# A transformer block on one core: the half-head attention product moved next to the modulation rows, and the last output chunk cut into two pieces in place of three

## The chip, the cores and the metric

The kernel runs on one core of one Trainium2 chip. The metric is the device time of one execution in microseconds. Every run whose state is on record is in the fast state, with a mean granted clock of the tensor engine of 0.999 or 1.0. PE is the tensor engine, PEld its weight loads, DVE the vector engine, ACT the scalar engine, POOL the general engine and SP the engine that issues most of the DMA transfers (SPq is its queue).

The *span* of a run goes from its first to its last instruction in the profile. The *time outside the span* is the measured time less the span.

## The reference

```python
B, N, D = (2, 256, 1152)          # two sequences of 256 tokens, H = 2 heads of 576, F = 4 * D
mod = (_silu(c) @ w_mod).reshape(B, 6, 1, D)
shift_a, scale_a, gate_a, shift_m, scale_m, gate_m = [mod[:, i] for i in range(6)]
h = _layernorm(x, axis=-1) * (1 + scale_a) + shift_a
qkv = (h @ wqkv).reshape(B, N, 3, H, Dh)
q, k, v = ...
attn = _softmax(jnp.einsum('bqhd,bkhd->bhqk', q, k) * Dh ** (-0.5), axis=-1)
a = jnp.einsum('bhqk,bkhd->bqhd', attn, v).reshape(B, N, D) @ wo
x = x + gate_a * a
h2 = _layernorm(x, axis=-1) * (1 + scale_m) + shift_m
m = _gelu(h2 @ w_fc1) @ w_fc2
return x + gate_m * m
```

A head has 576 columns, four blocks of 128 and one half block of 64. The two half blocks share columns 512 to 639 of V: that is the "half-head" part.

## The kernel before

The kernel has its own list scheduler. PE's units run in the order in which the program lists them; the other engines' units are placed by it. `mm` is a matmul, `S.unit` opens a unit, `dma` issues a transfer, on SP unless told otherwise. These are the parts that the change touches, and what it moves them around (cuts are marked with `...`):

```python
# issue loop: the waits for older stores stand ahead of the LAST store
outs = [ins for u in order["sp"] for ins in u.instrs if ins.is_out]
last_out = outs[-1]
...
        if ins is last_out:
            for o in outs[:-4]:
                eng_handle.wait_ge(dma_sems[o.dma_sem], o.dma_val)
        bi = ins.fn(eng_handle)
...

def v_proj(t, ci):                       # V for 128 tokens and 384 columns: 9 matmuls
    ...
    for kt in range(KT):
        mm(o, HX[:, kt, t*128:(t+1)*128], WV[:, kt, ci*CH:(ci+1)*CH], kt == 0, kt == KT-1)
    copy_on("act", V[:, t, ci*CH:(ci+1)*CH], o, ...)

def rows():                              # modulation rows, tiles of 32 columns
    for kt in range(KT):
        for r in range(2):
            for j in range(4):
                mm(psum[32*j:32*j+2, ...], ST[:, kt:18:9], WMODR[...], ..., tile_position=(0, 32*j))
    ...                                  # copy out, store to DRAM, load the gate back on all partitions

def pv_halves():                         # half-head P x V, tiles of 64 columns
    for b in range(2):
        for kjt in range(2):
            for h in range(2):
                base = PVB[b][2] * 512
                mm(psum[64*h:64*h+64, base:base+256], V[:, 2*b+kjt, 512+64*h:576+64*h],
                   PTS[2*b+h][:, kjt, :], kjt == 0, kjt == 1, tile_position=(0, 64*h))
    ...                                  # two copies out of PSUM to OT

# order of the units on PE
... v_proj(2, 0); rows(); ... v_proj(2, 1); v_proj(2, 2); v_proj(3, 0); rows_T(); v_proj(3, 1); v_proj(3, 2); ...
pv_halves()
for b in range(2):
    for h in range(2):
        pv(b, h)                         # the full-width part of P x V
...

# second feed-forward product, the output; CH = 384, JT = 36
for t in range(4):
    pieces = [(0, CH), (CH, 2*CH), (2*CH, 3*CH)]
    if t == 3:
        pieces = [(0, CH), (CH, 2*CH), (2*CH, 3*CH-160), (3*CH-160, 3*CH-64), (3*CH-64, 3*CH)]
    for (c0, c1) in pieces:
        for j in range(JT):
            mm(o, GT[j][:, t*128:(t+1)*128], WFC2[:, j, c0:c1], j == 0, j == JT-1)
        # DVE: times the gate, plus x1; then the store
        ...
```

Of the kernel before, what the change touches and what calls it, by code (L numbers as in the profile page):

```python
# [171 lines left out]
class Sched:  # L172
# [225 lines left out]
    def emit(self, nc, sems, dma_sems):  # L398
# [64 lines left out]
        outs = [ins for u in order["sp"] for ins in u.instrs if ins.is_out]  # L463
        last_out = outs[-1]

        def run_engine(e, eng_handle):
            for u in order[e]:
                for ins in u.instrs:
                    for (k, v) in waits[ins.gidx]:
                        if k[0] == "d":  # L470
                            eng_handle.wait_ge(dma_sems[k[1]], v)
                        else:
                            eng_handle.wait_ge(sems[k[1]], v)
                    if ins is last_out:
                        for o in outs[:-4]:
                            eng_handle.wait_ge(dma_sems[o.dma_sem], o.dma_val)
                    bi = ins.fn(eng_handle)
                    if ins.dma_sem is not None:
                        bi.then_inc(dma_sems[ins.dma_sem], 16)
                    else:  # L480
                        bi.then_inc(sems[e], 1)
            if e == "sp":
                for o in outs[-4:-1]:
                    eng_handle.wait_ge(dma_sems[o.dma_sem], o.dma_val)
                eng_handle.wait_ge(dma_sems[last_out.dma_sem], last_out.dma_val)
# [21 lines left out]
CH = 384  # L507
# [34 lines left out]
def build_kernel(nc, x, c, wqkv, wo, w_mod, w_fc1, w_fc2, out):  # L542
# [5 lines left out]
    with (  # L548
# [377 lines left out]
        def proj(W, j, dst_j, H, bank):  # L926
            S.unit("pe", KT * c_mm(512), "qk_%d" % dst_j)
            for kt in range(KT):
                mm(ps32(bank), W[:, kt, j * 128:(j + 1) * 128], H[:, kt, :], kt == 0, kt == KT - 1)
            qk_evac(dst_j, bank)  # L930
# [84 lines left out]
        def pt_transposes(b, h):  # L1015
            idx = b * 2 + h
            bank = s_bank[(b, h)]
            S.unit("pe", 4 * c_mm(128), "PT_%d_%d" % (b, h))
            for kjt in range(2):
                for jq in range(2):  # L1020
                    tr(ps16(bank, kjt * 256 + jq * 128, 128), PP[idx][:, jq, kjt * 128:(kjt + 1) * 128], IDENT)
            copy_on("dve" if b == 0 else "act", PTS[idx].rearrange("p j k -> p (j k)"), ps16(bank, 0, 512), 512, True, "PT_ev%d" % idx)
# [4 lines left out]
        def v_proj(t, ci):  # L1027
            bank = v_banks[v_rr[0] % 3]
            v_rr[0] += 1
            S.unit("pe", KT * c_mm(CH), "v_%d_%d" % (t, ci))  # L1030
            o = ps32(bank, 0, CH)
            for kt in range(KT):
                mm(o, HX[:, kt, t * 128:(t + 1) * 128], WV[:, kt, ci * CH:(ci + 1) * CH], kt == 0, kt == KT - 1)
            copy_on("act", V[:, t, ci * CH:(ci + 1) * CH], o, CH, False, "v_ev%d_%d" % (t, ci))
# [5 lines left out]
        def rows():  # L1040
            S.unit("pe", KT * 2 * c_mm(RW) + 100.0, "rows")
# [3 lines that stand above are left out]
                        c0 = 2 * RW * j + RW * r  # L1045
                        bank = (3, 4)[r]
                        mm(psum[32 * j:32 * j + 2, bank * 512:bank * 512 + RW], ST[:, kt:18:9], WMODR[:, kt, c0:c0 + RW],
                           kt == 0, kt == KT - 1, tile_position=(0, 32 * j))
            for r, eng in ((0, "act"), (1, "dve")):
                copy_on(eng, ROWS[0:98, ROWP + r * RW:ROWP + (r + 1) * RW], ps32(3 + r, 0, RW)[0:98, :], RW, False, "rows_ev%d" % r)  # L1050
            for j in range(2):
                dma(scratch[0, :, 2 * RW * j:2 * RW * (j + 1)], ROWS[32 * j:32 * j + 2, ROWP:ROWP + 2 * RW], 2 * 2 * RW * 2, "st_ga%d" % j, eng="pool")
            gate_load(0, GA)
# [58 lines left out]
        def pv_halves():  # L1112
            S.unit("pe", 4 * c_mm(256) + 100.0, "PVh")
# [3 lines that stand above are left out]
                        base = PVB[b][2] * 512  # L1117
                        mm(psum[64 * h:64 * h + 64, base:base + 256], V[:, 2 * b + kjt, 512 + 64 * h:576 + 64 * h], PTS[2 * b + h][:, kjt, :],
                           kjt == 0, kjt == 1, tile_position=(0, 64 * h))
            for b, eng in ((0, "dve"), (1, "act")):  # L1120
                copy_on(eng, OT[:, 4, b * 256:(b + 1) * 256], ps32(PVB[b][2], 0, 256), 256, False, "OT_ev%d_4" % b)

# [84 lines left out]
        proj(WQ, 7, 7, HX, 1)  # L1207
        s_and_softmax(1, 0)
        proj(WQ, 8, 8, HX, 2)
        v_proj(0, 0)  # L1210
        s_and_softmax(0, 1)
        v_proj(0, 1)
        s_and_softmax(1, 1)
        v_proj(0, 2)
        pt_transposes(0, 0)
        v_proj(1, 0)
        pt_transposes(1, 0)
        v_proj(1, 1)
        pt_transposes(0, 1)
        v_proj(1, 2)  # L1220
        pt_transposes(1, 1)
        v_proj(2, 0)
        rows()
        wfc1_load(0)
        wfc1_load(1)
        v_proj(2, 1)
        v_proj(2, 2)
        v_proj(3, 0)
        rows_T()
        v_proj(3, 1)  # L1230
        v_proj(3, 2)
        wfc1_load(2)
        wfc1_load(3)

# [3 lines left out]
        dma(WGM, wmod_v[:, :, 5 * D:6 * D], D * D * 2, "ld_gm", run=2304)  # L1238
        wfc2_load(0)
        wfc2_load(1)  # L1240
        pv_halves()
        for b in range(2):
            for h in range(2):
                pv(b, h)
# [26 lines left out]
        for t in range(4):  # L1271
            b = t // 2
            pieces = [(0, CH), (CH, 2 * CH), (2 * CH, 3 * CH)]
            if t == 3:
                pieces = [(0, CH), (CH, 2 * CH), (2 * CH, 3 * CH - 160), (3 * CH - 160, 3 * CH - 64), (3 * CH - 64, 3 * CH)]
            for (c0, c1) in pieces:
                w = c1 - c0
                S.unit("pe", JT * c_mm(w), "fc2_%d_%d" % (t, c0))
                o = ps32(acc_bank(), 0, w)
                for j in range(JT):  # L1280
                    mm(o, GT[j][:, t * 128:(t + 1) * 128], WFC2[:, j, c0:c1], j == 0, j == JT - 1)
                gm, t1, ost, x1c = GM[b][:, c0:c1], T1[oi % 3][:, 0:w], OST[oi % 3][:, 0:w], X1[:, t, c0:c1]
                oi += 1
                dve(c_dve_psum32(w), lambda e, o=o, gm=gm, t1=t1: e.tensor_tensor(out=t1, in0=o, in1=gm, op=ALU.mult), [o, gm], [t1], "fc2_t1_%d_%d" % (t, c0))  # L1284
                dve(c_dve_32(w), lambda e, t1=t1, x1c=x1c, ost=ost: e.tensor_tensor(out=ost, in0=t1, in1=x1c, op=ALU.add), [t1, x1c], [ost], "fc2_out_%d_%d" % (t, c0))  # L1285
                dma(outv[b, :, t % 2, c0:c1], ost, P * w * 2, "st_out_%d_%d" % (t, c0), is_out=True)
# [74 lines left out]
```

## Time and profile before

| | before |
|---|---|
| time, median of 3 runs | 243.87 us (243.79 to 244.35) |
| time of the profiled run, and its span | 243.62 us, 242.3 us |
| PE busy | 238.4 us, 98% |
| last pieces, PE time (DVE start to DVE start) | 224 columns 3.45, 96 columns 1.53, 64 columns 1.23 us |
| start of the first long PE stage (K products) | 11.18 us after the span's start |

In a timeline a line reads: start, length, engine, source line, operation, shape out and in, count, and in square brackets the idle time of the engine before it with what ended that.

### The profile page before, as it was taken

To read this page: it belongs to the slowest core of one execution; us is meant where nothing else is said; L and a number is where in the kernel's file an instruction comes from. 1 tells how busy PE (TensorE), PEld (TensorE's weight loads), DVE (VectorE), ACT (ScalarE), POOL (GpSimd) and SP (SyncE) were. 2 spreads that over 40 slices of the span, in tenths; PEclk is the share of its full clock that TensorE was granted. 3 is DMA by queue.
4 is the path that set the end of the run, shared out by engine and by line. 5 is a ranking of instruction groups with operands and counts; after the bars stand their busy time and mean duration, and the time that the engine had idled before them with its cause. 6 is when DMAs were issued, how large, how long until landed. Compare 5 with 4: busy or idle time off the path is not lost.

```text
span 242.3 us, 4076 instructions
## 1 busy us (share of the span) xinstructions
PE 238.4 (98%) x1763; PEld 147.5 (61%) x1763; DVE 120.3 (50%) x218; ACT 67.0 (28%) x136; POOL 21.2 (9%) x39
## 2 busy tenths in 40 slices
PE   7999999999999999999999999999999999999996
PEld 2698854556667666898444444444566656656676
DVE  3814388696997699789999500000022222111112
ACT  5820350355424107973233322222000000000000
POOL 1400000000021186400000000020000000000000
PEclk9999999999999999999999999999999999999999
DMA  6999999999996999989953498012000000000001
GB/s 241 330 381 392 391 392 391 397 413 405 391 356 196 351 395 391 391 266 394 314 164 82 150 320 313 0 29 72 0 16 19 16 16 19 16 16 16 19 24 27
DMA packets 30140, 51.59 MB, mean 213 GB/s; under 512 B 1703, under 2 KB 15787, under 8 KB 30123
## 3 DMA queue, kind: packets, MB, share of 16 engines
q1 hardware_dynamic: 29680, 50.14, 58.0%
q0 software_dynamic: 416, 1.19, 1.6%
q8 instruction: 14, 0.23, 0.4%
q14 instruction: 3, 0.02, 0.0%
q10 hardware_dynamic: 27, 0.00, 0.0%
HBM read 50.14 MB, written 1.19 MB: 212 GB/s over the span
## 4 chain that ended last, share of the span: by engine, by line
PE 97%; DVE 2%; POOL 0%; issue 0%; ACT 0%; DVEq 0%; POOLq 0%
PE psum L688 95%; PE psum L691 2%; DVE arena L739 1%; DVE arena L760 0%; POOL arena L711 0%; DVE arena L740 0%; DVE arena L1284 0%; DVE arena L1285 0%; POOL arena L710 0%; ACT arena L726 0%; DVE arena L727 0%; DVE arena L732 0%; DVE arena L742 0%; POOL arena L717 0%; POOL arena L715 0%
## 5 line engine op out<-in xcount | busy, mean ns | idle before, releaser
L688 PE MATMUL psum<-arena 128*128 128x384 bf16 (+10 forms) x1674 | 234.9, 306 | 1.6 <-POOL arena L711 1.5
L688 PEld LDWEIGHTS psum<-arena 128*128 128x128 bf16 (+3 forms) x1674 | 142.3, 97 | 90.0 <-issue 3.8
L1079 DVE SCALAR_TENSOR_TENSOR arena<-arena 128x1152 f32<-128x1152 bf16 x32 | 44.7, 1414 | 0.6
L1284 DVE TENSOR_TENSOR arena<-psum,arena 128x384 f32<-128x384 f32 (+3 forms) x14 | 7.0, 501 | 68.0 <-PE psum L688 68.0
L1193 ACT ACTIVATE arena<-psum 128x512 bf16<-128x512 f32 (+1 forms) x44 | 22.4, 520 | 42.7 <-PE psum L688 42.7
L683 ACT ACTIVATE arena<-psum 128x512 bf16<-128x512 f32 (+6 forms) x37 | 19.6, 549 | 39.5 <-PE psum L688 37.1
L685 DVE CAST arena<-psum 128x512 bf16<-128x512 f32 (+3 forms) x13 | 8.2, 641 | 11.4 <-PE psum L688 11.3
L669 POOL DMA_DIRECT2D dit_scratch<-arena x3 | 1.8, 616 | 115.7 <-DVE arena L685 58.9
L1161 POOL TENSOR_TENSOR arena<-arena 128x384 f32<-128x384 f32 x12 | 10.9, 910 | 10.8 <-DVE arena L1160 9.5
L1106 DVE CAST arena<-psum 72x32 bf16<-72x32 f32 x1 | 0.2, 186 | 21.3 <-PE psum L688 21.3
L739 DVE BATCH_NORM_STATS2 arena<-arena 128x6 f32<-128x384 f32 (+1 forms) x18 | 9.5, 552 | 0.1
L1166 ACT ACTIVATE arena<-arena 128x1152 bf16<-128x1152 f32 x4 | 5.3, 1345 | 11.9 <-DVE arena L1165 11.9
L691 PEld LDWEIGHTS psum<-arena 128*128 128x128 bf16 (+1 forms) x89 | 5.8, 98 | 2.5 <-issue 0.8
L1160 DVE TENSOR_TENSOR arena<-psum,arena 128x384 f32<-128x384 f32 x12 | 6.5, 549 | 1.6 <-DMA arena<-dit_scratch 1.6
L1285 DVE TENSOR_TENSOR arena<-arena 128x384 bf16<-128x384 f32 (+3 forms) x14 | 7.0, 501 | 0.5
L691 PE MATMUL psum<-arena 128*128 128x128 bf16 (+1 forms) x89 | 7.1, 219 | 0.1
L1180 DVE TENSOR_SCALAR arena<-psum,arena 128x128 bf16<-128x128 bf16 x20 | 5.4, 341 | 1.9 <-PE psum L691 1.9
L1183 ACT ACTIVATE arena<-psum,arena 128x128 bf16<-128x128 bf16 x16 | 6.0, 456 | 0.9 <-PE psum L688 0.6
L1086 DVE TENSOR_REDUCE arena<-arena 128x36 f32<-128x1152 f32 x4 | 5.4, 1348 | 0.0
L1083 DVE STREAM_TRANSPOSE arena<-arena 128x1152 f32<-128x1152 f32 x4 | 5.4, 1364 | 0.0
L1009 ACT ACTIVATE arena<-psum,arena 128x256 bf16<-128x256 f32 x8 | 3.7, 472 | 1.3 <-PE psum L688 0.9
L743 POOL TENSOR_TENSOR arena<-arena 128x1 f32<-128x1 f32 x6 | 3.6, 596 | 2.0 <-DVE arena L742 2.0
(48 smaller groups left out, 44.9 us busy)
## 6 DMA issues: line engine op xcount, KB each, us to landing
arena<-in_w_fc_dram SPq DMA_DIRECT2D x9, 1152.0 KB, 7.3
arena<-in_w_fc_dram SPq DMA_DIRECT2D x4, 2592.0 KB, 17.2
arena<-in_wqkv_dram SPq DMA_DIRECT2D x18, 288.0 KB, 10.2
arena<-in_w_mod_dram SPq DMA_DIRECT2D x3, 1728.0 KB, 20.2
arena<-in_w_mod_dram SPq DMA_DIRECT2D x3, 864.0 KB, 13.7
arena<-in_w_mod_dram SPq DMA_DIRECT2D x9, 288.0 KB, 10.5
arena<-in_wqkv_dram SPq DMA_DIRECT2D x1, 2592.0 KB, 16.6
arena<-in_wo_dram SPq DMA_DIRECT2D x1, 2592.0 KB, 24.4
```

Of the source, the lines that this page charges most:

```text
L683: act(c_act(n), lambda e: e.activation(out=dst, in_=src, func=ACTF.Copy), [src], [dst], name)
L685: dve(c_dve_psum16(n) if psum16 else c_dve_psum32(n), lambda e: e.tensor_copy(dst, src), [src], [dst], name)
L688: S.instr(lambda e: e.matmul(o, lhsT=l, rhs=r, start=st, stop=sp, **kw), reads=[l, r], writes=[o])
L691: S.instr(lambda e: e.transpose(o, i_, idn), reads=[i_, idn], writes=[o])
L739: dve(550, lambda e, s=s, o=o: e.bn_stats(out=o, in_=s), [s], [o], "bn_%s_%d" % (tag, ci))
L1079: dve(1270, lambda e, w=w, s=s, acc=acc: e.scalar_tensor_tensor(out=acc, in0=w, scalar=s, in1=acc, op0=ALU.mult, op1=ALU.add), [w, s, acc] ...
L1160: dve(550, lambda e, o=o, ga=ga, x1c=x1c: e.tensor_tensor(out=x1c, in0=o, in1=ga, op=ALU.mult), [o, ga], [x1c], "wo_t1_%d_%d" % (t, ci))
L1161: S.op("pool", 930, lambda e, xs=xs, x1c=x1c: e.tensor_tensor(out=x1c, in0=x1c, in1=xs, op=ALU.add), reads=[x1c, xs], writes=[x1c], name=" ...
L1183: act(440, lambda e, o=o, dst=dst, s1=s1, s2=s2: e.activation(out=dst, in_=o, func=ACTF.Identity, scale=s1, bias=s2), [o, s1, s2], [dst], ...
L1193: act(c_act(ntok), lambda e: e.activation(out=dst, in_=o, func=ACTF.Gelu_apprx_tanh), [o], [dst], "gelu_%d_%d" % (f, tok0))
L1284: dve(c_dve_psum32(w), lambda e, o=o, gm=gm, t1=t1: e.tensor_tensor(out=t1, in0=o, in1=gm, op=ALU.mult), [o, gm], [t1], "fc2_t1_%d_%d" % ( ...
L1285: dve(c_dve_32(w), lambda e, t1=t1, x1c=x1c, ost=ost: e.tensor_tensor(out=ost, in0=t1, in1=x1c, op=ALU.add), [t1, x1c], [ost], "fc2_out_%d ...
```

## The change

The intent: the two stages in which PE works in column tiles are put side by side, so that PE switches its tiling fewer times. For that the columns of V that the half-head product reads are made first. The last output chunk is cut once, not twice, which saves 36 matmuls. The waits for older stores go ahead of the second-last store, so that they don't lie between the last two.

```diff
@@ issue loop
-                    if ins is last_out:
+                    if ins is outs[-2]:
                         for o in outs[:-4]:
                             eng_handle.wait_ge(dma_sems[o.dma_sem], o.dma_val)
@@ pv_halves
+
+        def pv_halves_ev():
             for b, eng in ((0, "dve"), (1, "act")):
                 copy_on(eng, OT[:, 4, b * 256:(b + 1) * 256], ps32(PVB[b][2], 0, 256), 256, False, "OT_ev%d_4" % b)
@@ order of the units (cut: the softmax and transpose units, which keep their slots, and the removed lines of the moved v_proj and rows_T)
+        v_proj(0, 1)
+        v_proj(1, 1)
+        v_proj(2, 1)
+        v_proj(3, 1)
         v_proj(0, 0)
 ...
         v_proj(2, 0)
+        pv_halves()
         rows()
         wfc1_load(0)
         wfc1_load(1)
+        v_proj(3, 0)
+        v_proj(0, 2)
+        v_proj(1, 2)
+        rows_T()
         v_proj(2, 2)
         v_proj(3, 2)
+        pv_halves_ev()
 ...
-        pv_halves()
@@ output pieces of the last token tile
-                pieces = [(0, CH), (CH, 2 * CH), (2 * CH, 3 * CH - 160), (3 * CH - 160, 3 * CH - 64), (3 * CH - 64, 3 * CH)]
+                pieces = [(0, CH), (CH, 2 * CH), (2 * CH, 3 * CH - 64), (3 * CH - 64, 3 * CH)]
```

More of the change, by code (lines that the diff above doesn't have):

```diff
@@ L1209, in build_kernel @@
         proj(WQ, 8, 8, HX, 2)
-        v_proj(0, 0)
-        s_and_softmax(0, 1)
-        v_proj(0, 1)
-        s_and_softmax(1, 1)
-        v_proj(0, 2)
-        pt_transposes(0, 0)
+        v_proj(0, 1)
+        s_and_softmax(0, 1)
+        v_proj(1, 1)
+        s_and_softmax(1, 1)
+        v_proj(2, 1)
+        pt_transposes(0, 0)
+        v_proj(3, 1)
+        pt_transposes(1, 0)
+        v_proj(0, 0)
+        pt_transposes(0, 1)
         v_proj(1, 0)
-        pt_transposes(1, 0)
-        v_proj(1, 1)
-        pt_transposes(0, 1)
-        v_proj(1, 2)
         pt_transposes(1, 1)
         v_proj(2, 0)
+        pv_halves()
         rows()
@@ L1225, in build_kernel @@
         wfc1_load(1)
-        v_proj(2, 1)
+        v_proj(3, 0)
+        v_proj(0, 2)
+        v_proj(1, 2)
+        rows_T()
         v_proj(2, 2)
-        v_proj(3, 0)
-        rows_T()
-        v_proj(3, 1)
         v_proj(3, 2)
+        pv_halves_ev()
         wfc1_load(2)
```

## The prediction

> **What bounds the kernel now.** I read the page first (busy shares, slices, chain), then the timeline of the last six microseconds, then the weight-load timeline around the two places where the PE works in column tiles, then the groups and timelines that say how much slack the other engines have. From the page:
>
> ```profile
> PE 238.4 (98%) x1763; PEld 147.5 (61%) x1763; DVE 120.3 (50%) x218; ACT 67.0 (28%) x136; POOL 21.2 (9%) x39
> ...
> PE   7999999999999999999999999999999999999996
> ...
> PEclk9999999999999999999999999999999999999999
> ...
> PE 97%; DVE 2%; POOL 0%; issue 0%; ACT 0%; DVEq 0%; POOLq 0%
> ```
>
> The span is 242.3 us. PE is busy in every slice but the first and the last, at full granted clock, and the chain that ended last is 97% PE. So the time is the sum of the PE's stream, plus a start that the change does not touch, plus a tail after the last matmul. Moving PE work to another place gains nothing by itself. The change can gain only by making the stream shorter or the tail shorter, and it can lose only by making the PE wait where it does not wait now.
>
> The tail, from the timeline (start, length, engine, line, shape, idle time before):
>
> ```profile
> 237.55 0.39 DVE L1284 TENSOR_TENSOR arena<-psum,arena 128x224 f32<-128x224 f32 x1 [2.30 <-PE psum L688]
> ...
> 239.08 0.26 DVE L1284 TENSOR_TENSOR arena<-psum,arena 128x96 f32<-128x96 f32 x1 [0.71 <-PE psum L688]
> ...
> 240.31 0.22 DVE L1284 TENSOR_TENSOR arena<-psum,arena 128x64 f32<-128x64 f32 x1 [0.68 <-PE psum L688]
> 240.57 0.22 DVE L1285 TENSOR_TENSOR arena<-arena 128x64 bf16<-128x64 f32 x1
> ```
>
> The 384-piece before these starts its DVE work at 234.10. DVE start to DVE start gives the PE time of each piece: 224 columns 3.45 us, 96 columns 1.53 us, 64 columns 1.23 us, each for 36 matmuls, so 95.8, 42.5 and 34.2 ns a matmul. A 384-piece takes 5.85 us, 162.5 ns a matmul. After the last matmul come two DVE operations (done at 240.79), the issue of the last store at 240.82, and its landing: the view of DMA issues gives 1.4 us for the 16 KB store, which lands near 242.2. That is the end.
>
> The waits for older stores sit in the kernel between the second-last and the last store. The view of that line:
>
> ```profile
> L476 SPq EVENT_SEMAPHORE  x5: 28/28/28, 240.0 to 240.3; - x5
> ```
>
> They run from 240.0 to 240.3, half a microsecond before the store can be issued at all, because its data come at 240.79. They are hidden now, so moving them gains nothing by itself.
>
> The two column-tiled stages, from the timeline of weight loads:
>
> ```profile
> 65.57 2.06 PEld L688 LDWEIGHTS psum<-arena 128*2 128x2 bf16 x72 [0.32 <-issue]
> 67.88 0.28 PEld L688 LDWEIGHTS psum<-arena 128*128 128x128 bf16 x3 [0.25 <-issue]
> ...
> 75.55 0.36 PEld L688 LDWEIGHTS psum<-arena 128*64 128x64 bf16 x8 [0.32 <-issue]
> 76.10 0.22 PEld L688 LDWEIGHTS psum<-arena 128*128 128x128 bf16 x3 [0.20 <-issue]
> ```
>
> The modulation rows are the 128*2 loads, the half-head PV is the 128*64 loads. Each has a gap before it and after it in which no weights are loaded, put down to no other engine. In the matmul starts the same shows as 256 ns where 162.5 is normal (65.314 to 65.570 and 75.292 to 75.548), so 94 ns lost on entry. On the way out of the half-head PV there are 205 ns after the last pair where pairs come 110 apart: 95 ns again. Out of the rows it is about 95 too (2.31 us for 18 groups of four that come 122.5 ns apart leaves 105). So the trace has four such losses, some 0.38 us in all.
>
> **What the Trainium skill says.** "TensorEngine Tiling (Array Packing)", Key Properties: "Mode switching requires drain: Changing tiling mode (not just tile) drains the TensorE". The trace agrees, with 94 to 105 ns for each of the four switches. The page lists 128x64 and 128x32 as different configurations, so a switch between them should drain too; no place in this trace shows that one. "TensorE: Matmul & The Clock Gate", Back-to-back issue gap, gives N/2.4 + 2.5 ns when warm: 95.8, 42.5 and 162.5 for 224, 96 and 384 columns, exactly as measured; 64 columns measured 34.2 from DVE to DVE, against 29.2. "DMA: Bandwidth & Descriptors", Specifications, has a line-rate minimum of 512 B, below which a read-modify-write is done. Stores of 224, 96 and 64 columns have rows of 448, 192 and 128 B; 320 columns would be 640 B. The trace has 3.3 us to landing for the 56 KB store against 1.6 us for 96 KB, but its packets show one straggler doing that, with fifteen of sixteen landings within 1.5 us, so I do not lean on this.
>
> **The change part by part.**
>
> *Order of the V products.* The same 12 units of 9 matmuls with 384 columns (9 x 162.5 = 1.46 us each), the same softmax and transpose units between them in the same slots, the same rotation of three banks. Cost 0. All it does is to make V's columns 512 to 639 ready early, so that the half-head PV can run before the rows.
>
> *Half-head PV next to the rows.* The eight matmuls stay. Before: full to 32-tile, to full, to 64-tile, to full: four drains. After: full to 64-tile, to 32-tile, to full: three drains if a switch between tile sizes drains, two if not. Gain 95 ns, at most 190. I take 0.10 us. Its last operand, the fourth transposed probability tile, is copied by ACT until 64.97; the PE would arrive at 65.48 plus the drain. Half a microsecond of slack, so no new wait. The two copies out of PSUM must stay behind the last V product, since their output overlays the normalized input that V reads; the banks they hold meanwhile (6 and 7) are used by nobody before.
>
> *Pieces 224 + 96 become 320.* 36 matmuls fewer. 320 columns take 95.8 + 96 x 0.417 = 135.8 ns, so 36 x 135.8 = 4.89 us in place of 3.45 + 1.53 = 4.98. Gain 0.09 us, all on the path, as the DVE waits for PE there (0.68 to 2.30 us idle before each piece).
>
> *Tail after the last matmul.* With T the DVE start of the last piece, the 320-piece starts on DVE at T - 1.23. Between 0.39 us for 224 columns and 0.56 us for 384, an operation of 320 columns is estimated at 0.49, so two end at T - 0.2. Its store occupies the queue's issuer for 0.33 us, until about T + 0.2. The last store is issued at T + 0.51 as before, and ends 1.4 us later. The 80 KB store has landed by about T + 1.5. So the last store still sets the end and the tail stays at 2.0 us. If the five waits had stayed where they are they would run from T + 0.2 to nearly T + 0.6 and reach past T + 0.51; moved ahead of the 320-piece, they lie in its long idle time. The move protects about 0.1 us rather than gains it.
>
> Sum: 243.87 - 0.10 - 0.09 = 243.68 us.
>
> **The rivals.** *First, a new wait at the gate rows.* The rows now start 0.47 us later (half-head PV without its exit drain), while everything after PV comes 0.1 us earlier. The rows feed a store to DRAM and a broadcast load of the first gate, and there DVE waits:
>
> ```profile
> 69.32 1.25 POOL L669 DMA_DIRECT2D dit_scratch<-arena  x2 [58.92 <-DVE arena L685]
> 75.97 1.13 POOL L669 DMA_DIRECT2D arena<-dit_scratch  x2 [5.40 <-DMA dit_scratch<-arena]
> ...
> 83.32 0.56 DVE L1160 TENSOR_TENSOR arena<-psum,arena 128x384 f32<-128x384 f32 x1 [1.56 <-DMA arena<-dit_scratch]
> ...
> 91.02 1.35 ACT L1166 ACTIVATE arena<-arena 128x1152 bf16<-128x1152 f32 x1 [10.61 <-DVE arena L1165]
> ...
> 92.95 0.44 PE L691 MATMUL psum<-arena 128*128 128x128 bf16 x5
> ```
>
> The gate's arrival starts a chain over DVE and POOL that ends with the normalized rows on ACT at 92.37; PE transposes them at 92.95. Slack 0.58, less 0.10 to 0.19 of PE gain, so 0.4 to 0.5. If the gate came the full 0.47 us later, PE would stand still for 0 to 0.1 us; if the reordered DVE list puts one more 1.33 us operation ahead of the rows' copy, it could be 0.8 to 0.9. Against it: the store's 5.4 us are mostly queueing behind weight loads (DMA share above 1.0 until 73, then 0.16 at 74.5 to 75.0), so a store issued later should land at nearly the same time. I give one in four to a loss here, up to 0.9 us: 243.7 to 244.6. PSUM is no limit: the first bank would be wanted back near 85.4 and is free at 83.9.
>
> *Second, the tile-to-tile switch is free:* 243.58. One in five.
>
> *Third, the end is set by the 320-store, not the last one.* Three earlier stores had a single packet ring land 0.5 to 1.6 us late, when a 16 KB instruction fetch sat on one DMA engine (one began at 239.4). With 72 PE instructions fewer at the end this fetch should fall away, or move well before the last two stores. If it hits instead, the end moves by up to 1.3 us: 245. One in twenty.
>
> *Fourth, the gain is much larger than I see,* because the author expected the store waits to be on the path. The trace speaks against it.
>
> **Range and chances.** The sure terms are about 0.2 us, the first rival adds about 0.1 us on average, and the three runs of the kernel before lie within 0.56 us. I predict 243.7 us, with 8 in 10 for 243.3 to 244.2. Two per cent is 4.9 us: no rival reaches it. Faster 0.01, within 2% 0.98, slower 0.01.
>
> **What would show it.** Right: the 128*64 and 128*2 weight loads stand side by side, with three idle gaps about them in all; PE stays gapless from there to the end; DVE start of the 320-piece to that of the 64-piece is 1.23 us, and from the 384-piece before it 4.89 us; the waits of the queue lie before the 320-store; from the last DVE start to the end 2.0 us. Wrong: a weight load waiting on ACT near 92 to 94 us, a gap before the first transposes, a first gate multiplication after 83.8, or a last store later than 0.51 us after the last piece's DVE start.

## The result

The changed kernel takes **244.35 us** (median of 5 runs, 244.05 to 244.67). The kernel before takes 244.02 us in the same rounds (243.79 to 244.35). The ratio is 1.0011 with a 95% interval of 0.9996 to 1.0026. A ratio is the mean time of one kernel's fast runs over the mean of the other's fast runs of the same rounds, so it is not quite the ratio of the medians. The number is above the predicted range, and on the other side of the kernel before from the one predicted.

The page of the changed kernel, the lines that answer to those shown of before:

```profile
PE 238.1 (98%) x1717; PEld 146.5 (60%) x1727; DVE 120.0 (49%) x216; ACT 67.1 (28%) x136; POOL 21.8 (9%) x39
...
PE   7899999999999999999999999999999999999996
...
PE 94%; DMA 3%; SPq 1%; issue 0%; DVE 0%
PE psum L688 93%; DMA arena<-in_w_mod_dram 3%; PE psum L691 2%; SPq L669 1%; DVE arena L1287 0%; DVE arena L1288 0%
```

There are 36 weight loads fewer (1763 to 1727); the 1717 matmuls are less than that because some records are missing from the trace. PE is busy in every slice but the first and the last, as before. What is new is in the chain: 3% of the span, at its beginning, is a weight transfer (`in_w_mod_dram`) that PE waited for.

The weight-load timeline of the changed kernel where PE works in tiles:

```profile
66.45 0.36 PEld L688 LDWEIGHTS psum<-arena 128*64 128x64 bf16 x8 [0.32 <-issue]
67.00 2.06 PEld L688 LDWEIGHTS psum<-arena 128*2 128x2 bf16 x72 [0.20 <-issue]
...
69.31 0.28 PEld L688 LDWEIGHTS psum<-arena 128*128 128x128 bf16 x3 [0.25 <-issue]
```

The 64-column loads and the 2-column loads stand side by side, with three gaps about them where there were four.

The last microseconds, from the timeline of DVE, and the waits for older stores (their place in SP's program, when they ran):

```profile
235.46 0.56 DVE L1288 TENSOR_TENSOR arena<-arena 128x384 bf16<-128x384 f32 x1
239.76 0.49 DVE L1287 TENSOR_TENSOR arena<-psum,arena 128x320 f32<-128x320 f32 x1 [3.74 <-PE psum L688]
...
240.99 0.23 DVE L1287 TENSOR_TENSOR arena<-psum,arena 128x64 f32<-128x64 f32 x1 [0.21 <-PE psum L688]
```

```profile
L476 SPq EVENT_SEMAPHORE  x5: 17/28/28, 236.4 to 236.7; - x5
```

The 384-piece's first DVE operation starts at 234.87, so the 320-piece follows 4.89 us later and the 64-piece 1.23 us after that, both as predicted. The waits now lie in DVE's idle time before the 320-piece. The last store is issued at 241.50, 0.51 us after the last piece's DVE start.

**Where the time went.** The starts of certain matmuls in the two traces cut the span into stages whose edges the change does not move (us):

| stage | before | after | after less before |
|---|---|---|---|
| span's start to first K product | 11.184 | 12.061 | +0.877 |
| first K product to first V product | 41.415 | 41.417 | +0.002 |
| first V product to the scale columns (V, rows, half-head PV, PV, part of the projection) | 37.250 | 37.143 | -0.107 |
| scale columns to the second gate's rows | 67.951 | 67.951 | 0 |
| second gate's rows to the second feed-forward product | 11.749 | 11.749 | 0 |
| second feed-forward product to the 64-piece | 69.330 | 69.240 | -0.090 |
| 64-piece, first to last matmul | 1.020 | 1.020 | 0 |
| last matmul to the span's end | 2.445 | 2.373 | -0.072 |
| span | 242.34 | 242.95 | +0.61 |
| measured time less span | 1.28 | 1.72 | +0.44 |
| measured time | 243.62 | 244.67 | +1.05 |

So what the change was meant to gain is there, 0.107 and 0.090 us. In this one execution it is outweighed by two things that no line of the change speaks of: a later start of the K products, and a longer time outside the span. The page shows the first only as the 3% in its chain, and the second not at all.

The start, from PE's timeline. The 128x2 products are the scale columns, 128x256 are the K products. Before:

```profile
8.49 1.33 PE L688 MATMUL psum<-arena 128*128 128x2 bf16 x26
...
10.32 0.47 PE L688 MATMUL psum<-arena 128*128 128x2 bf16 x12
...
11.18 0.49 PE L688 MATMUL psum<-arena 128*128 128x256 bf16 x3
```

After:

```profile
8.63 0.69 PE L688 MATMUL psum<-arena 128*128 128x2 bf16 x13
9.54 0.47 PE L688 MATMUL psum<-arena 128*128 128x2 bf16 x12 [0.21 <-DMA arena<-in_w_mod_dram]
...
11.08 0.47 PE L688 MATMUL psum<-arena 128*128 128x2 bf16 x12 [0.33 <-DMA arena<-in_w_mod_dram]
...
12.06 0.49 PE L688 MATMUL psum<-arena 128*128 128x256 bf16 x3
```

PE's matmuls waited 0.21 and 0.33 us for weights, which they did not before; its weight loads waited 0.51 and 0.50 us for the same transfers, against 0.23 and 0.17. The trace shows why in this run: of the 16 rings of the first transfer from w_mod, 14 had landed at 7.07 us, and two at 8.09 and 8.14. The three loads that the scale columns need then landed at 8.14, 9.49 and 11.03, against 7.99, 9.07 and 10.28 before.

### The profile page after: what moved, and what is told of

It is laid out like the page before. It is cut to its first block, busy times and chain, and to the rows that moved or that the text cites. A ratio compares the mean times of both kernels' runs of the same rounds, so it can differ in the third digit from the quotient of the medians.

```text
span 243.0 us, 3989 instructions
## 1 busy us (share of the span) xinstructions
PE 238.1 (98%) x1717; PEld 146.5 (60%) x1727; DVE 120.0 (49%) x216; ACT 67.1 (28%) x136; POOL 21.8 (9%) x39
## 3 DMA queue, kind: packets, MB, share of 16 engines
q0 software_dynamic: 416, 1.19, 1.7%
HBM read 50.14 MB, written 1.19 MB: 211 GB/s over the span
## 4 chain that ended last, share of the span: by engine, by line
PE 94%; DMA 3%; SPq 1%; issue 0%; DVE 0%
PE psum L688 93%; DMA arena<-in_w_mod_dram 3%; PE psum L691 2%; SPq L669 1%; DVE arena L1287 0%; DVE arena L1288 0%
## 5 line engine op out<-in xcount | busy, mean ns | idle before, releaser
L688 PE MATMUL psum<-arena 128*128 128x384 bf16 (+9 forms) x1628 | 234.6, 310 | 2.6 <-POOL arena L711 1.5
L688 PEld LDWEIGHTS psum<-arena 128*128 128x128 bf16 (+1 forms) x1638 | 141.2, 97 | 92.0 <-issue 4.1
L1287 DVE TENSOR_TENSOR arena<-psum,arena 128x384 f32<-128x384 f32 (+2 forms) x13 | 6.8, 526 | 68.3 <-PE psum L688 68.3
L691 PEld LDWEIGHTS psum<-arena 128*128 128x128 bf16 (+1 forms) x89 | 5.8, 98 | 2.2 <-DMA arena<-in_c_dram 0.8
L1288 DVE TENSOR_TENSOR arena<-arena 128x384 bf16<-128x384 f32 (+2 forms) x13 | 6.8, 527 | 0.5
```

The costliest lines, as they stand in the source:

```text
L688: S.instr(lambda e: e.matmul(o, lhsT=l, rhs=r, start=st, stop=sp, **kw), reads=[l, r], writes=[o])
L691: S.instr(lambda e: e.transpose(o, i_, idn), reads=[i_, idn], writes=[o])
L1287: dve(c_dve_psum32(w), lambda e, o=o, gm=gm, t1=t1: e.tensor_tensor(out=t1, in0=o, in1=gm, op=ALU.mult), [o, gm], [t1], "fc2_t1_%d_%d" % ( ...
L1288: dve(c_dve_32(w), lambda e, t1=t1, x1c=x1c, ost=ost: e.tensor_tensor(out=ost, in0=t1, in1=x1c, op=ALU.add), [t1, x1c], [ost], "fc2_out_%d ...
```

## The experiments

Two questions were open. Is the late start the change's doing, or chance? And what makes the time outside the span longer? Theory A for the first: the program up to the K products is the same, so the start is chance, which differs from one execution to the next. Rival B: the changed program has a longer start in every execution, for instance because its instructions lie elsewhere in memory. For the second: theory C, the end of the execution depends on the program of some engine; rival D, it is chance as well.

### Both kernels again

**before_again** and **after_again** are the two kernels without an edit, for the spread of both numbers.

> The kernel before, unchanged, against itself. Both theories: ratio 1.000; what I want is the spread. My theory (the head of the program, until the first K products start, depends on when the first pieces of w_mod land, and that varies from run to run): single runs differ by 0.3 to 0.6 us, and the K products of this profile start anywhere between 11.0 and 12.2 us, not at exactly 11.18; from their start to the end the trace has 231.2 us again, within 0.05. Rival (the head is fixed for a given program): they start at 11.2 within 0.1, and the spread comes from elsewhere.

> The changed kernel, unchanged. My theory: from the start of the K products to the end 231.0 us, 0.2 us less than in the kernel before, as in its first trace; the head is drawn anew, so the start lies anywhere between 11.0 and 12.2 us and the total is 243.5 to 244.4, ratio 0.998 to 1.001. Rival (the change lengthens the head, say by where the program lies in memory): start at 12.0 or later again, ratio 1.001 or more.

Measured, with 5 rounds: before_again 244.01 us (243.91 to 244.16), ratio 0.9986 (0.9969 to 1.0003); after_again 244.44 us (244.0 to 244.7), ratio 1.0002 (0.9982 to 1.0022). The kernel before ran beside them at 244.31 us in the median of 11 runs, between 243.66 and 245.22: a spread of 1.56 us for one program.

The K products started at 11.223 us in before_again and at 11.676 in after_again. The same changed program had 12.061 in its first trace. So the start moves by 0.39 us without any edit, and that part is theory A. The spans of all runs agree, with a trace or without: their mean is 242.68 us in the six runs of after_again and 242.92 in the 17 runs of the kernel before and before_again of the same rounds, so the changed kernel shows no later start on average. The time at which PE reaches its full granted clock varies too, 4.97 us in before, 7.30 in before_again, 5.55 in after_again, but these are not in the order of the starts, so that it sets the start is not shown. From K products to the end it is 231.464 and 231.016 us. Of the difference of 0.448, the two stages of the change are 0.197, as in the first traces; 0.22 is a longer end of before_again (2.596 us from the last matmul). So the expectation of 231.2 for before_again, within 0.05, was missed.

The time outside the span was another matter: 1.31 to 1.41 us in every run of before_again, 1.70 to 1.77 in every run of after_again. That is not chance, so rival D falls here.

### An attempt to take the chance out of the start: more warming matmuls

**before_pad** and **after_pad** add PE work that needs no data just ahead of the second transpose unit, so that PE comes to the scale columns after their weights have landed.

```diff
         for n, behind in ((1, "bn_ln1_1_1"), (1, "aggr_ln1_1"), (2, "veps_ln1_1"), (2, "rstd_ln1_1")):
             warm(n, behind, behind)
+        warm(14, "pad")
         xn_T(1)
```

> The kernel before with 14 more warm-up matmuls, 3.0 us of PE, ahead of the first transposes, so that all loads of the head have landed by the time PE wants them. My theory: total up by 2.1 to 3.0 us (ratio 1.009 to 1.012), no PE wait on w_mod, and single runs within 0.2 us of each other. Rival (spread from elsewhere): total up by 3.0 and the spread stays at 0.5 us.

> The changed kernel with the same 14 matmuls. My theory: 0.19 us faster than the kernel before with the padding, within 0.1, and as tight. Rival (the change costs 0.3 us in the head whatever the loads do): 0.1 to 0.3 us slower than the kernel before with the padding.

Measured: before_pad 246.5 us (246.37 to 246.95), ratio 1.0093; after_pad 246.58 us (246.28 to 247.24), ratio 1.0095. The expectation of a small spread failed (0.58 and 0.96 us). So did that of a gain: the changed one is 0.08 us slower, not 0.19 faster. In the traces the K products start at 13.738 and 14.461. The pad exchanged one chance for another, as its length depends on when the full clock is granted: the 512-column matmuls go from 427 to 216 ns apart near 5.0 us in before_pad and at 7.74 in after_pad. The time outside the span was 1.28 to 1.38 against 1.68 to 1.74 (one run 2.03).

### Holding the start for all engines

**before_hold**, **after_hold**, **latewait_hold** and **narrow_hold** let the first statistics on POOL wait for a chain of eleven additions there, whose length does not hang on PE's clock, and let PE warm meanwhile.

```diff
+        HOLD = SMA[:, 0:CH]
+        S.op("pool", 20, lambda e: e.memset(HOLD, 0.0), writes=[HOLD], name="hold_0")
+        for i in range(1, 12):
+            S.op("pool", 20, lambda e: e.tensor_tensor(out=HOLD, in0=HOLD, in1=HOLD, op=ALU.add), reads=[HOLD], writes=[HOLD], name="hold_%d" % i)
-        warm(7, "b")
+        warm(29, "b")
+        # and mm_ln1*, var_ln1*, rstd_ln1* on POOL ordered after hold_11
```

latewait_hold is after_hold with the waits for older stores ahead of the last store again (`if ins is last_out:`). narrow_hold is after_hold with the half-head PV in the same 32-column tiles as the rows:

```diff
-                    for h in range(2):
+                    for j in range(4):
                         base = PVB[b][2] * 512
-                        mm(psum[64 * h:64 * h + 64, base:base + 256], V[:, 2 * b + kjt, 512 + 64 * h:576 + 64 * h], PTS[2 * b + h][:, kjt, :],
-                           kjt == 0, kjt == 1, tile_position=(0, 64 * h))
+                        mm(psum[32 * j:32 * j + 32, base:base + 256], V[:, 2 * b + kjt, 512 + 32 * j:544 + 32 * j], PTS[2 * b + j // 2][:, kjt, :],
+                           kjt == 0, kjt == 1, tile_position=(0, 32 * j))
```

> The kernel before with POOL held for some 10 us by eleven additions on a spare tile ahead of the first layer norm, and 22 more warm-up matmuls so that PE keeps working meanwhile. By then all early loads have landed and the PE clock is up, so both things that I suspect of the varying head (late rings of the w_mod loads; the moment at which the clock is released, seen at 5.0 to 7.7 us) end before anything waits for them. My theory: total up by 4 to 7 us, but single runs within 0.25 us of each other; start of the K products to the end 231.2 us. Rival (spread from elsewhere): spread of 0.5 us as before.

> The changed kernel with the same hold. My theory (the change saves 0.107 us between PV and rows and 0.090 us in the last pieces, and the rest of the measured difference was the head): 0.20 us faster than the kernel before with the hold, within 0.1. Rival (the change itself lengthens the head by 0.3 to 0.6 us): slower than it by 0.1 us or more, with the K products starting later.

> The changed kernel with the hold, but with the waits for older stores back ahead of the last store. My estimate in the prediction: the five waits run after the issue of the 320-store and reach 0.05 to 0.1 us past the moment when the last piece's data are ready, so the last store is issued at 0.56 to 0.6 us after the last piece's DVE start in place of 0.51. Rival (hidden, moving them was needless): issue at 0.51 to 0.52 as in the changed kernel.

> The changed kernel with the hold and with the half-head PV cut into 16 matmuls of 32 columns, four side by side, so that it works in the same tile mode as the rows that follow. If the loss between them is a drain for the change of tile mode: the 202 ns seen after the last pair become 110 and the stage is 0.09 us shorter than in the changed kernel. If every change of operands in tile mode costs it, or 32-column weight loads cost more: no gain, or a loss of up to 0.1 us.

Measured, with 5 rounds:

| run | median (lowest to highest), us | K products start | K products to end | time outside the span |
|---|---|---|---|---|
| before_hold | 248.74 (248.70 to 248.78) | 15.959 | 231.199 | 1.50 to 1.58 |
| after_hold | 249.56 (249.31 to 249.62) | 15.958 | 231.580 | 2.01 to 2.06 |
| latewait_hold | 249.67 (249.26 to 249.87) | 16.380 | 231.475 | 1.97 to 2.06 |
| narrow_hold | 248.90 (248.86 to 248.97) | 15.961 | 230.891 | 1.97 to 2.07 |

The hold did its work: three of four start within 3 ns of each other. Given the same moment of data, the changed kernel starts its K products when the one before does. Together with the spans above, that leaves nothing for rival B. But after_hold is 0.82 us slower than before_hold, which nobody expected. Two terms make it up. The time outside the span is about 0.49 longer. And the last stores took longer. The view of DMA issues of after_hold (size in KB, us from issue to landing):

```profile
out_dram<-arena SPq DMA_DIRECT2D x1, 80.0 KB, 2.3
...
out_dram<-arena SPq DMA_DIRECT2D x1, 16.0 KB, 2.0
```

The same lines of the changed kernel itself:

```profile
out_dram<-arena SPq DMA_DIRECT2D x1, 80.0 KB, 1.6
...
out_dram<-arena SPq DMA_DIRECT2D x1, 16.0 KB, 1.4
```

In after_hold an instruction fetch of 16,384 bytes began at 244.791 us, just before the 80 KB store was issued, and took 1.26 us. Fifteen of that store's sixteen parts had landed by 246.39 us, the last at 247.13; last matmul to end became 2.959 us in place of 2.381 in before_hold. That the fetch lay in front of the store's packets on one DMA engine is read from these times; no record names the engine. narrow_hold agrees: its fetch began 0.6 us earlier, at 244.18, and its end is 2.380 us. This is the third rival of the prediction, caused here by the experiment's own additional PE instructions. In the changed kernel itself the last such fetch is at 225.3, in the kernel before at 239.4: there it moved away from the end as the prediction said. 0.49 + 0.58 less the 0.20 of gain is 0.87, against 0.82 measured.

latewait_hold started 0.42 us late after all, so its total says nothing. Its last store was issued 0.57 us after the last piece's DVE start, against 0.513 in after_hold. By this one pair of traces, moving the waits is worth 0.055 us.

narrow_hold answers whether a switch from 64- to 32-column tiles drains PE. The weight-load timeline of narrow_hold:

```profile
70.45 2.50 PEld L688 LDWEIGHTS psum<-arena 128*32 128x32 bf16 x88 [0.32 <-issue]
73.20 0.76 PEld L688 LDWEIGHTS psum<-arena 128*128 128x128 bf16 x6 [0.25 <-issue]
```

And of after_hold:

```profile
70.44 0.36 PEld L688 LDWEIGHTS psum<-arena 128*64 128x64 bf16 x8 [0.32 <-issue]
71.00 2.06 PEld L688 LDWEIGHTS psum<-arena 128*2 128x2 bf16 x72 [0.20 <-issue]
```

With the narrow tiles the gap of 0.20 us between the two groups is gone, though there are eight matmuls more. The stage from V to the scale columns fell from 37.144 to 37.035 us, by 0.109.

### Which part of the change lengthens the time outside the span

**mid_only** is the changed kernel with the old pieces and the old place of the waits. **tail_only** is the kernel before with the new pieces and the new place of the waits. **two_stores** is the changed kernel, but the 320-piece is stored by two transfers, as many stores as before:

```diff
-                dma(outv[b, :, t % 2, c0:c1], ost, P * w * 2, "st_out_%d_%d" % (t, c0), is_out=True)
+                cut = 224 if w == 320 else w
+                dma(outv[b, :, t % 2, c0:c0 + cut], ost[:, 0:cut], P * cut * 2, "st_out_%d_%d" % (t, c0), is_out=True)
+                if cut < w:
+                    dma(outv[b, :, t % 2, c0 + cut:c1], ost[:, cut:w], P * (w - cut) * 2, "st_out_%d_%db" % (t, c0), is_out=True)
```

**two_waits** is the changed kernel with two more waits on SP, for two loads that landed at the beginning, so they stop nothing:

```diff
                     if ins is outs[-2]:
                         for o in outs[:-4]:
                             eng_handle.wait_ge(dma_sems[o.dma_sem], o.dma_val)
+                        for o in [i for v in order["sp"] for i in v.instrs][:2]:
+                            eng_handle.wait_ge(dma_sems[o.dma_sem], 16)
```

> The change of order alone; the last chunk and the store waits as in the kernel before (14 stores, 80 instructions on the DMA-issuing engine). In all runs so far the measured time less the span of the instructions is 1.22 to 1.41 us for the kernel before, but 1.68 to 1.77 for the changed one (one run of the padded one 2.03), a fixed 0.4 us that no instruction of the kernel shows. If it belongs to the last part of the change: here 1.3 us, and a total of 243.9 to 244.2. If it belongs to the order of PE's work: 1.7. The stage from the first V product to the end of PV is 0.107 us shorter than before in either case.

> The pieces of 320 and 64 and the moved store waits alone; 13 stores, 79 instructions on the DMA-issuing engine. If the 0.4 us belongs to this part: time less span 1.7 us, and 0.3 us slower than the order alone. If to the order: 1.3. The last chunk is 0.090 us shorter in either case.

> The changed kernel, but the 320-piece is stored by two DMAs of 224 and 96 columns: 14 stores and 80 instructions on the DMA-issuing engine again, with the DVE and PE work of the changed kernel. If the 0.4 us comes with the number of stores or of that engine's instructions: time less span is back at 1.3 us, and the kernel is 0.2 to 0.4 us faster than the changed one and 0.2 faster than the kernel before. If it comes with DVE's shorter program or PE's: 1.7 us.

> The changed kernel with two more waits, on the first two loads, which were met 230 us before, at the place of the store waits: they are paired into one more instruction of the DMA-issuing engine (80 again) while the stores stay 13. If the number of that engine's instructions counts: time less span 1.3 us, total 243.6 to 244.1. If the number of stores counts: 1.7 us.

Measured, with 3 rounds, beside the kernel before at 244.11 us:

| run | median (lowest to highest), us | ratio (95%) | time outside the span |
|---|---|---|---|
| mid_only | 243.79 (243.76 to 243.95) | 0.9993 (0.9972 to 1.0013) | 1.27 to 1.40 |
| tail_only | 244.37 (244.33 to 244.75) | 1.0018 (0.9999 to 1.0036) | 1.71 to 1.75 |
| two_stores | 244.38 (244.21 to 244.59) | 1.0015 (0.9997 to 1.0033) | 1.26 to 1.31 |
| two_waits | 243.79 (243.59 to 243.90) | 0.9990 (0.9972 to 1.0008) | 1.20 to 1.30 |

The longer end comes with the pieces, not with the order of V or PV. (tail_only moves the waits as well, but latewait_hold, with the waits moved back, has the longer end too.) It does not come with the number of pieces, of stores or of DVE operations, because two_waits has all of these as the changed kernel does, and has lost the longer end. What two_waits and two_stores share is one more instruction on SP. two_waits and tail_only ran in the same rounds and their ranges do not overlap: 0.58 us between the medians. That is what the parts give: some 0.46 outside the span and 0.107 in the V stage.

two_stores was expected to be faster in total by the same token and was not: its last matmul to end was 2.94 us in the trace, with three stores close together at the end. The time outside the span did what was expected of it.

### Is it a count, and does the place matter

**sp81** and **sp82** wait for the first four and the first six loads in place of two (`[:4]`, `[:6]`). In the trace two such waits count as one instruction, so these have 81 and 82 on SP. **early80** is as two_waits, but with the two waits early, ahead of the load of the output projection's weights. **best** puts the narrow half-head PV and the two added waits together.

```diff
+                    if e == "sp" and ins.name == "ld_wo":      # early80
+                        for o in [i for v in order["sp"] for i in v.instrs][:2]:
+                            eng_handle.wait_ge(dma_sems[o.dma_sem], 16)
```

> The changed kernel with four more waits that are long met, 81 instructions on the DMA-issuing engine. If odd numbers cost 0.4 us at the end: time less span 1.7 us. If anything from 80 up is free of it: 1.3 us, total 243.6 to 244.1.

> The changed kernel with six more such waits, 82 instructions. Parity: 1.3 us. From 80 up free: 1.3 us. A period of four or more: may be 1.7 us.

> The changed kernel with the two extra waits 190 us earlier, ahead of the load of the output projection's weights, where they are long met; 80 instructions. If the number counts: time less span 1.3 us. If only an instruction at the end helps: 1.7 us.

> The changed kernel with both repairs: the extra instruction on the DMA-issuing engine and the half-head PV in 32-column tiles (0.11 us shorter in the run with the hold). From the first K products to the end 230.9 us, time less span 1.3 us, so 0.31 us faster than the kernel before and 0.6 to 0.7 us faster than the changed one: 243.5 to 243.9 with the head as it falls, ratio 0.998 to 0.999.

Measured beside the kernel before at 243.74 us (11 runs): sp81 243.51 us, ratio 0.9989 (0.9970 to 1.0008); sp82 244.36, ratio 1.0021 (1.0002 to 1.0039); early80 243.90, ratio 0.9999 (0.9979 to 1.0019); best 243.58 (243.41 to 243.74, 6 runs), ratio 0.9990 (0.9973 to 1.0006).

The next table sets SP's instruction count, as the traces have it, beside the end of the run. The third column is the first semaphore update after the last instruction, from the trace's records of such updates. It is of a semaphore that no instruction of the program names, and is taken here for the start of the end barrier.

| kernels | instructions on SP | first update after the span, us | time outside the span, us |
|---|---|---|---|
| after, after_again, tail_only | 79 | 0.60 to 0.62 | 1.67 to 1.78 |
| before, two_stores | 80 | 0.16 to 0.18 | 1.22 to 1.41, 1.26 to 1.31 |
| mid_only, two_waits, early80, best | 80 | 0.14 | 1.20 to 1.40 |
| sp81 | 81 | 0.11 | 1.18 to 1.26 |
| sp82 | 82 | 0.12 | 1.19 to 1.27 |

So 79 instructions cost 0.4 to 0.5 us at the end, and 80, 81 and 82 do not. It isn't parity, and early80 shows that the place of the added instruction doesn't matter. That an added instruction on PE or POOL would do as well is ruled out by the kernels with the pad and the hold, which add such: the first update still comes at 0.61 us with 79 on SP (after_pad and the three with the change and the hold) and at 0.14 with 80 (before_pad, before_hold). sp82 is slower in total for another reason: in its trace its K products started at 11.890 and its last store came 0.44 us late, and its span was 243.1 to 243.2 in all four runs.

best has the second-lowest median of its rounds, behind sp81. By its parts it should be the fastest: the V stage at 37.035 us is 0.215 below the kernel before, the pieces give 0.090, and the time outside the span is that of before. By the times alone it is not told apart from the kernel before, as its interval holds 1; and the changed kernel did not run in these rounds.

**What the kept traces add on the cause.** In all 18 traces an instruction fetch of 8,192 bytes starts near the end, 1.04 to 1.07 us after the end of SP's 79th recorded instruction (1.25 in after, 1.33 in narrow_hold), whatever that instruction is: the last wait with 79 on SP, the wait before it with 80, the last store with 81, the store before it with 82. And where SP has a next instruction, it starts no sooner than 0.40 to 0.42 us after the 79th: in before, before_again and two_stores the last wait ends 0.05 to 0.09 us after the last store has landed, in place of 0.02 in the others. So SP seems to pause for some 0.4 us behind its 79th instruction. With 80 or 81 the pause lies under a wait for a store, with 82 it holds up the last store's issue by 0.04 us, and with 79 nothing covers it and the end barrier comes later. This fits every row of the table, but it is read from the traces; no run was made to test it. In sp82 the fetch, at 242.02 us, also falls between the last store's issue at 241.37 and its landing: fifteen of its sixteen parts landed by 242.86, the last at 243.18. That the fetch held it back is likely and not tested.

**What stays open.** Why SP pauses there, if it does, and what counts below 79 or above 82 would do. The kernels with the hold have 0.23 us more again outside the span (1.54 and 2.03 in place of 1.31 and 1.73); the first update comes no later there, so it lies elsewhere, and that was not looked into. In early80's trace PE also lost 0.354 us in the middle, which is taken up below; why the gate came late in that run and not in the others was not tried.

## Why the prediction was wrong

**The step that failed** is the sum, "243.87 - 0.10 - 0.09 = 243.68 us". It lists every term of PE's stream and takes everything else as fixed: "a start that the change does not touch, plus a tail after the last matmul", and, of the last store, "which lands near 242.2. That is the end." The measured time does not end there. There are 1.3 us outside the span in the kernel before and 1.7 in the changed one, and this term, missing from the sum, measured +0.42 us (1.73, the mean of its five runs, less 1.31, the mean of 38 runs of the kernel before in the later rounds). Both numbers of the kernel before, 243.62 and 242.3, were there to be read; that their difference could depend on the program was not.

What is left of the miss is smaller. The median was 244.35, 0.67 above 243.68. Besides the 0.42, the base was 0.15 low (243.87 from three runs, 244.02 in the rounds in which the two were compared). The tail was 0.07 better than assumed, nearly all of it because in the kernel before the last wait ended 0.083 us after the last store had landed and in the changed one 0.017. That leaves about 0.17 for the start, which differs by more than that between executions of one program. Only one of these five executions has a trace, so this last part is worked out as a remainder and not shown.

- **Drains**, "I take 0.10 us" for one fewer: right, 0.107 measured in the stage. The drain between the two tile sizes was the doubtful one; it is there (202 ns after the last pair in the changed kernel, where pairs come 110 apart), and narrow_hold took it away for another 0.109. The second rival, a free switch, fell.
- **Pieces**, 0.09 us: right, 0.090 measured, with 4.89 and 1.23 us for the two as worked out. One reading was wrong without effect: the 64-column piece's 34.2 ns a matmul. Its 36 matmuls start within 1.020 us, so they come 29.1 ns apart, close to the 29.2 that the prediction set against it; the rest of the 1.23 us lies behind its last matmul.
- **Tail**, "stays at 2.0 us": DVE start of the last piece to the end of the span is 1.96 us, the store issued at 0.51. The move of the waits was put at about 0.1 us protected; latewait_hold measured 0.055.
- **The first rival**, a wait at the gate, one in four: it did not come in the changed kernel's traces. Its timelines:

```profile
70.76 1.25 POOL L669 DMA_DIRECT2D dit_scratch<-arena  x2 [59.86 <-DVE arena L685]
...
76.47 1.13 POOL L669 DMA_DIRECT2D arena<-dit_scratch  x2 [4.46 <-DMA dit_scratch<-arena]
...
82.66 0.56 DVE L1162 TENSOR_TENSOR arena<-psum,arena 128x384 f32<-128x384 f32 x1
...
90.96 1.35 ACT L1168 ACTIVATE arena<-arena 128x1152 bf16<-128x1152 f32 x1 [9.78 <-DVE arena L1167]
...
93.72 0.39 PE L691 MATMUL psum<-arena 128*128 128x128 bf16 x4
```

The store of the rows is issued 1.44 us later than before (of which 0.88 is the later start; the remaining 0.56, in place of the 0.47 predicted, includes the drain between the two tile sizes, which that sum left out), but it waits 4.46 us to be landed in place of 5.40, so the gate load is issued only 0.50 later. The first gate multiplication waits for PE alone, the normalized rows are done at 92.31, and PE transposes them at 93.72 with a slack of 1.41 us. The argument against this rival, that most of the store's time was queueing, agrees with that. The rival was rightly called one in four and not nothing, though: in the trace of early80 the gate came late enough.

```profile
76.69 1.13 POOL L672 DMA_DIRECT2D arena<-dit_scratch  x2 [5.12 <-DMA dit_scratch<-arena]
...
84.14 0.56 DVE L1165 TENSOR_TENSOR arena<-psum,arena 128x384 f32<-128x384 f32 x1 [2.04 <-DMA arena<-dit_scratch]
...
93.23 0.54 PEld L694 LDWEIGHTS psum<-arena 128*128 128x128 bf16 x9 [0.18 <-ACT arena L1171]
```

There the first gate multiplication starts at 84.14, past the 83.8 that the prediction named as the sign, and PE's weight load waits for ACT. The stage from the scale columns to the second gate's rows is 68.305 us long in that trace in place of 67.951, so 0.354 us were lost. In the other traces compared by stages it was not lost, the two of the changed kernel among them.

- **The third rival**, an instruction fetch on the last stores, one in twenty: in the changed kernel the fetch fell away from the end as expected. That it costs about 0.6 us when it hits, after_hold shows.
- **The range** was too narrow for another reason too: it was drawn from three runs that lie within 0.56 us. The start alone differed by 0.39 us between two traces of the changed kernel, and the kernel before spread over 1.56 us in eleven runs.

## What to carry to other kernels

When a change is worth tenths of a microsecond, take the measured time apart into the stages of the stream, the start and the time outside the span, for several runs of both kernels, before you believe any of them to be fixed. A gain that the trace shows to the nanosecond in its own stage can still be lost where no engine line stands: here one instruction fewer on the DMA-issuing engine cost twice what the change gained. And an experiment that adds instructions moves the instruction fetches too, so look where they land before you read its total.

## What the Trainium skill lacked or had wrong

- "Runtime: NRT & Kernel Launch", The ~15µs preamble/postamble breakdown, gives the ending barrier one figure, some 1.5 us, the time until all engines are done. No page says that it depends on how many instructions an engine has. Here the time outside the span, which is not the same quantity, was 1.67 to 1.78 us with 79 instructions on the DMA-issuing engine and 1.18 to 1.41 us with 80 to 82, in the kernels without pad or hold, and the first semaphore update of the end came 0.60 us after the last instruction against 0.11 to 0.18.
- "Runtime: NRT & Kernel Launch", Instruction fetch mechanics, has blocks of 16 KiB and a cost of crossing one that is mostly hidden. The traces have packets of 16,384 bytes, and others of 8,192. No page gives what a fetch costs a transfer that it meets: in after_hold one came just before the last stores, and the 80 KB store took 2.3 us to landing in place of 1.6, the 16 KB store 2.0 in place of 1.4. Nor does a page say that a crossing can stand uncovered at the end of a program; the 0.4 us at 79 instructions may be one (not tested).
- "TensorEngine Tiling (Array Packing)", Key Properties, says that a change of tiling mode drains and gives no figure. Each such switch measured about 95 ns here. The page's drain holds for 64- to 32-column tiles as well: making both stages 32 columns wide saved 0.109 us.
- No page gives a figure for how much the start of a program's long stages moves by chance: the K products of one unedited program began at 12.061 and 11.676 us.
